# Moving 44 of 48 tile transposes from TensorE to the DMA engines, with a shorter layernorm, in a fused attention and MLP block

## The chip, the cores and the metric

One core of one Trainium2 chip runs the whole program. The metric is device microseconds from the first to the last instruction, as the runtime times an execution; the median of several executions is quoted. The profile's span is about 2 us shorter than that time (858.1 us beside 859.8 us).

## The reference, cut to what matters

```python
# x: 2048 x 1024, H = 32 heads of 32; bf16 everywhere
h  = x + linear_attention(layernorm(x), wqkv, wo)
#   q, k, v = layernorm(x) @ wqkv;  phi(t) = where(t > 0, t + 1, exp(t)) + 1e-6
#   kv = phi(k)^T v,  z = sum phi(k);  o = phi(q) kv / (phi(q) z + 1e-6);  o @ wo
h2 = h + (relu(n @ W_gate) * (n @ W_up)) @ W_down,   n = layernorm(h);   F = 3584
```

The matmuls of this kernel contract over partitions. The normalized `x`, the attention output and the normalized `h` come out with rows on partitions and must be turned, so that features lie on partitions, before the next matmul. That is 3 uses x 16 tiles of 128 x 1024 = 48 tile transposes.

## The kernel before

The kernel records its operations with the buffers that they read and write, and puts semaphore waits where they depend on another engine. A tile transpose is eight PE transposes of 128 x 128 into one PSUM bank and one copy out of it by ScalarE (ACT):

```python
def transpose8(src_ap, src_bufs, b, nblk, name):          # L461 in the profile of before
    tb = bank_bf(b)
    for i in range(nblk):
        PL.add("pe", lambda e, i=i: e.transpose(tb[:, i, :], src_ap[:, i*P:(i+1)*P], ident[:]), ...)
def evac_T(eng, b, nblk, dst_ap, dst_bufs, name):          # L469
    PL.add("act", lambda e: e.activation(out=dst_ap, in_=bank_bf(b)[:, 0:nblk, :], func=ACTF.Identity), ...)
```

`T1` turns the first layernorm's tiles (`xn` to `xnT`), `a3` the attention output (`osb` to `oT`), `a5` the second layernorm's tiles (`xn` to `hnT`). Between them, `a1` is a query projection, `a2` computes a tile's attention output, and `a4` its output projection, residual sum and second layernorm; `nop` is an empty place. Four stages follow one another:

```python
for st in range(WB): ...            # start: WB = 4 tiles, layernorm -> T1 -> first key projection
for st in range(WB, NST):           # projection: 12 steps
    T1(st + 1); ln1_norm(st + 2); ln1_stats(st + 3)
    trickle(2)                      # two of the later weight loads
    kvp(st); kvacc(st - 1)          # 32 matmuls of 512 columns, then 16 small ones
# first attention block: query projections a1 fill the gaps of this chain
chain = [("a2", 0), ("a2", 1), ("a2", 2), ("a3", 0), ("a2", 3), ("a3", 1), ("a4", 0), ("a3", 2),
         ("a4", 1), ("a3", 3), ("a5", 0), ("a4", 2), ("a5", 1), ("a4", 3), ("a5", 2), ("a5", 3)]
# MLP, 4 row blocks: gate/up units of 16 matmuls, with the next block's attention pieces between them,
# then two down-projection rounds
```

The layernorm takes mean and variance on VectorE (DVE), then three one-column operations on GpSimd (POOL), then normalizes on DVE. (In the cuts, SP is the engine that issues the DMA transfers.)

```python
pool: ve   = var + eps
pool: rstd = ve ** -0.5
pool: nmr  = mean * rstd * -1
dve:  xn   = x * rstd + nmr
```

## Time and profile before

| | before |
|---|---|
| median of 4 runs | 859.82 us (859.80 to 859.83) |
| profiled span | 858.1 us |
| TensorE busy / idle in the span | 845.4 us / 12.7 us |
| ACT, DVE busy | 174.2 us, 273.2 us |
| POOL busy, instructions | 35.6 us, 108 |
| DMA, mean | 128 GB/s |

A busy TensorE is not yet a bound, since matmuls overlap in the record (219 ns recorded for a transpose, 56 ns from one to the next).

### The profile page before, as it was taken

The page shows a single profiled execution, that of the slowest core. Times are in us where ns is not written, and L with a number is a line of the kernel's source. Part 1 is how long each engine was busy: PE and PEld are TensorE (multiplying, and loading weights), DVE is VectorE, ACT ScalarE, POOL GpSimd, SP SyncE. Part 2 cuts the span into 40 slices and gives each one's busy share as a digit, 9 for nine tenths or more (in the row PEclk, how much of TensorE's full clock was granted, in tenths as well). Part 3 has the DMA queues.
Part 4 walks back from the last instruction along what each step waited for, and adds up shares of the span by engine and source line. Part 5 has one row for each costly group of instructions (what it writes and reads, how often), then busy time and mean ns, then how long its engine had stood idle before and what let it go on. Part 6 is the DMA issues. An engine that isn't in the chain of part 4 may idle for free.

```text
span 858.1 us, 10919 instructions
## 1 busy us (share of the span) xinstructions
PE 845.4 (99%) x4538; PEld 407.1 (47%) x4627; DVE 273.2 (32%) x517; ACT 174.2 (20%) x262; POOL 35.6 (4%) x108
## 2 busy tenths in 40 slices
PE   7999999999999999999999999999999999999998
PEld 3555555544544444445444444544444444444443
DVE  6444524766433321124442101343411002112111
ACT  3344443324222210002222100022221001111100
POOL 3101100001000000000000000000000000000000
PEclk9999999999999999999999999999999999999999
DMA  9448100001233345553334465334344555363052
GB/s 295 135 147 272 61 2 1 1 13 38 89 121 123 111 160 183 177 166 99 123 123 148 147 196 173 122 112 151 97 157 154 189 173 163 107 197 98 29 170 95
DMA packets 105536, 109.75 MB, mean 128 GB/s; under 512 B 2960, under 2 KB 101520, under 8 KB 105488
## 3 DMA queue, kind: packets, MB, share of 16 engines
q1 hardware_dynamic: 105488, 109.06, 39.8%
q8 instruction: 36, 0.59, 0.3%
q14 instruction: 12, 0.10, 0.0%
HBM read 104.86 MB, written 4.19 MB: 127 GB/s over the span
## 4 chain that ended last, share of the span: by engine, by line
PE 96%; DVE 2%; issue 1%; POOL 1%; ACT 0%; DVEq 0%; ACTq 0%; POOLq 0%
PE ps L451 94%; PE ps L461 2%; DVE st L481 1%; POOL rstd L489 0%; DVE xn L504 0%; POOL nmr L492 0%; POOL ve L486 0%; DVE mv L484 0%; DVE RE L525 0%; DVE RF L693 0%; DVE RC L750 0%; ACT Et L520 0%; ACT RA L562 0%; POOL RF L344 0%; DVE RF L360 0%
## 5 line engine op out<-in xcount | busy, mean ns | idle before, releaser
L451 PE MATMUL ps<-RE,gring 128*128 128x512 bf16 x876 | 197.0, 379 | 1.2
L451 PE MATMUL ps<-RC,gring 128*128 128x512 bf16 x877 | 195.0, 379 | 1.0
L451 PE MATMUL ps<-wdring,RA 128*128 128x512 bf16 x877 | 193.0, 379 | 1.0
L723 ACT ACTIVATE RC<-ps 128x512 bf16<-128x512 f32 x112 | 66.9, 598 | 461.9 <-PE ps L451 461.9
L725 DVE TENSOR_TENSOR RA<-RC,ps 128x512 bf16<-128x512 bf16 x112 | 76.9, 687 | 262.1 <-PE ps L451 262.1
L451 PEld LDWEIGHTS ps<-wdring,RA 128*128 128x128 bf16 x896 | 87.7, 98 | 105.7
L451 PEld LDWEIGHTS ps<-RC,gring 128*128 128x128 bf16 x896 | 87.0, 98 | 102.9
L451 PEld LDWEIGHTS ps<-RE,gring 128*128 128x128 bf16 x896 | 86.4, 98 | 100.1
L451 PE MATMUL ps<-RB,RA 128*128 128x512 bf16 x496 | 111.3, 379 | 2.9 <-ACT RA L562 2.1
L451 PEld LDWEIGHTS ps<-RB,RA 128*128 128x128 bf16 x512 | 49.1, 98 | 58.8 <-ACT RA L562 2.6
L750 DVE TENSOR_TENSOR RC<-ps,RF 128x512 bf16<-128x512 f32 x32 | 20.1, 683 | 176.9 <-PE ps L451 176.9
L451 PE MATMUL ps<-wo,RE 128*128 128x512 bf16 x248 | 57.4, 379 | 0.4
L451 PE MATMUL ps<-RA,RC 128*128 128x512 bf16 x249 | 57.0, 379 | 0.4
L520 ACT ACTIVATE Et<-ps 128x512 bf16<-128x512 f32 x64 | 38.2, 597 | 84.7 <-PE ps L451 49.1
L522 DVE TENSOR_SCALAR E2t<-Et 128x512 bf16<-128x512 bf16 x64 | 18.5, 288 | 78.1 <-ACT Et L520 78.0
L451 PEld LDWEIGHTS ps<-wo,RE 128*128 128x128 bf16 x256 | 25.0, 98 | 30.2
L451 PEld LDWEIGHTS ps<-RA,RC 128*128 128x128 bf16 x256 | 24.3, 98 | 27.2
L693 DVE TENSOR_TENSOR RF<-ps,x 128x512 bf16<-128x512 f32 x32 | 22.1, 691 | 28.7 <-PE ps L451 28.5
L486 POOL TENSOR_SCALAR ve<-mv 128x1 f32<-128x1 f32 x32 | 7.1, 223 | 573.9 <-DVE mv L484 573.9
L469 ACT ACTIVATE RE<-ps 128x1024 bf16<-128x1024 bf16 x24 | 24.5, 1022 | 24.7 <-PE ps L461 24.7
L591 ACT ACTIVATE RE<-ps 128x512 bf16<-128x512 f32 x32 | 19.1, 597 | 36.3 <-PE ps L451 36.3
L525 DVE SCALAR_TENSOR_TENSOR RB<-ps,E2t 128x512 bf16<-128x512 f32 x32 | 22.1, 692 | 1.1
(50 smaller groups left out, 329.1 us busy)
## 6 DMA issues: line engine op xcount, KB each, us to landing
gring<-in_B_W_gate_dram SPq DMA_DIRECT2D x28, 1024.0 KB, 5.4
gring<-in_B_W_up_dram SPq DMA_DIRECT2D x28, 1024.0 KB, 7.5
wdring<-in_B_W_down_dram SPq DMA_DIRECT2D x56, 512.0 KB, 3.6
RB<-in_A_wqkv_dram SPq DMA_DIRECT2D x4, 1024.0 KB, 8.9
x<-in_A_x_dram SPq DMA_DIRECT2D x16, 256.0 KB, 2.6
out_dram<-RC SPq DMA_DIRECT2D x32, 128.0 KB, 3.6
RE<-in_A_x_dram SPq DMA_DIRECT2D x15, 256.0 KB, 2.8
RC<-in_A_wqkv_dram SPq DMA_DIRECT2D x2, 1024.0 KB, 6.8
```

The source lines that it names most:

```text
L451: lambda e: e.matmul(out_ap, lhsT, rhs, start=start, stop=stop, skip_group_check=skip),
L461: lambda e, i=i: e.transpose(tb[:, i, :], src_ap[:, i * P:(i + 1) * P], ident[:]),
L469: PL.add("act", lambda e: e.activation(out=dst_ap, in_=src, func=ACTF.Identity), reads=[B_bank[b]], writes=dst_bufs, name=name)
L481: PL.add("dve", lambda e, c=c: e.bn_stats(out=st6[:, k, c * 6:(c + 1) * 6], in_=src_full[:, c * BCH:(c + 1) * BCH]), reads=[src_chunk_bufs ...
L520: PL.add("act", lambda e: e.activation(out=Et[:, k, 0:w], in_=src, func=ACTF.Exp), reads=[B_bank[b]], writes=[B_E[k]], name=name + "_exp")
L522: PL.add("dve", lambda e: e.tensor_scalar(out=E2t[:, k, 0:w], in0=Et[:, k, 0:w], scalar1=1.0, scalar2=1e-6, op0=ALU.min, op1=ALU.add), rea ...
L525: PL.add("dve", lambda e: e.scalar_tensor_tensor(out=dst_ap, in0=src, scalar=C1, in1=E2t[:, k, 0:w], op0=ALU.add, op1=ALU.max), reads=[B_b ...
L591: PL.add("act", lambda e, b=b, j=j: e.activation(out=vv[:, slot, j * NW:(j + 1) * NW], in_=bank(b, NW), func=ACTF.Identity), reads=[B_bank ...
L693: PL.add("dve", lambda e, b=b, nt=nt: e.tensor_tensor(out=hsb[:, hs, j, nt * NW:(nt + 1) * NW], in0=bank(b, NW), in1=x2[:, xs, nt * NW:(nt ...
L723: PL.add("act", lambda e: e.activation(out=rg[:, k, :], in_=bank(ga, SBW), func=ACTF.Relu), reads=[B_bank[ga]], writes=[B_rg[k]], name="rg ...
L725: PL.add("dve", lambda e: e.tensor_tensor(out=hhT[:, ft, :], in0=rg[:, k, :], in1=bank(gb, SBW), op=ALU.mult), reads=[B_rg[k], B_bank[gb]] ...
L750: PL.add("dve", lambda e, j=j, k=k: e.tensor_tensor(out=outst[:, k, :], in0=bank(banks4[j], NW), in1=hsb[:, hs, j, dh * NW:(dh + 1) * NW], ...
```

## The change

The intent: take the transposes off the busiest engine, and give the layernorm a shorter path through POOL. Cut to its core:

```diff
-        NPK = 5
+        NPK = 4          # slots of phi(k) and v
+        NXN = 4          # slots of xn, 2 before
+        USE_DMA_T = True
...
-            PL.add("pool", ... ve = var + EPS)
+            PL.add("dve",  ... ve = var + EPS)
             PL.add("pool", ... rstd = ve ** -0.5)
-            PL.add("pool", ... nmr = mean * rstd * -1)
-            dve: xn = x * rstd + nmr
+            dve: xn = (x - mean) * rstd
...
+        def T1d(st):
+            PL.add("sp", lambda e: e.dma_start_transpose(xnT[:, :, st * P:(st + 1) * P], xn[:, k, :]), ...)
...     # a3, a5: the same with osb -> oT, xn -> hnT, issued right after a2 and a4
-        NDUM0, NDUM1 = 14, 5
+        NDUM0, NDUM1 = 12, 3      # warm-up matmuls
...     # projection, step st
-                T1(st + 1); ln1_norm(st + 2)
+                ln1_norm(st + 2); T1d(st + 2)
...     # first attention block
+            chain = [("a2", 0), ("a2", 1), ("a2", 2), ("a2", 3), ("nop", 0), ("nop", 0), ("nop", 0),
+                     ("a4", 0), ("a4", 1), ("a4", 2), ("a4", 3)]
+        tail_units = 8            # query projections kept for after the chain
...     # attention pieces between the MLP units
+                    order = [("a2", 0), ("a2", 1), ("a2", 2), ("a2", 3), ("nop", 0), ("nop", 0),
+                             ("a4", 0), ("a4", 1), ("a4", 2), ("a4", 3)]
```

The first four tiles (`st < WB`) keep their PE transposes. So 12 + 16 + 16 = 44 tile transposes move.

More of the change, by code (lines that the diff above doesn't have):

```diff
@@ L232, in bass_sequential_preLN__linear_attn_block__glu_gated_reglu__prompt_kernel @@
         jp_i = RF[:, 768:1024].bitcast(dt.int32)
-        xn = sb("xn", [P, 2, D], bf16)
+        xn = sb("xn", [P, NXN, D], bf16)
         Et = sb("Et", [P, 3, EW], bf16)
@@ L279, in bass_sequential_preLN__linear_attn_block__glu_gated_reglu__prompt_kernel @@
         sl_out = slots("dout_", NOS)
+        sl_tx = slots("dtx_", NXN)
+        sl_to = slots("dto_", NO)
         def bufs(name, n):
@@ L285, in bass_sequential_preLN__linear_attn_block__glu_gated_reglu__prompt_kernel @@
         B_x1 = [bufs("x1_%d_" % i, NBC) for i in range(NX1)]
-        B_xn = bufs("xn_", 2)
+        B_xn = bufs("xn_", NXN)
         B_xnT = [bufs("xnT%d_" % s_, 2) for s_ in range(NST)]
@@ L485, in layernorm @@
                    reads=B_st6[k], writes=[B_mv[k]], name=name + "_aggr")
-            PL.add("pool", lambda e: e.tensor_scalar(out=ve[:, k, :], in0=mv[:, k, 1:2], scalar1=EPS,
-                                                     scalar2=None, op0=ALU.add),
+            PL.add("dve", lambda e: e.tensor_scalar(out=ve[:, k, :], in0=mv[:, k, 1:2], scalar1=EPS,
+                                                    scalar2=None, op0=ALU.add),
                    reads=[B_mv[k]], writes=[B_ve[k]], name=name + "_ve")
@@ L491, in layernorm @@
                    reads=[B_ve[k], B_neghalf], writes=[B_rstd[k]], name=name + "_rstd")
-            PL.add("pool", lambda e: e.tensor_scalar(out=nmr[:, k, :], in0=mv[:, k, 0:1],
-                                                     scalar1=rstd[:, k, :], scalar2=-1.0,
-                                                     op0=ALU.mult, op1=ALU.mult),
-                   reads=[B_mv[k], B_rstd[k]], writes=[B_nmr[k]], name=name + "_nmr")
             def norm():
-                if norm_eng == "act":
-                    PL.add("act", lambda e: e.activation(out=dst_ap, in_=src_full, func=ACTF.Identity,
-                                                         scale=rstd[:, k, :], bias=nmr[:, k, :]),
-                           reads=list(src_chunk_bufs) + [B_rstd[k], B_nmr[k]], writes=[dst_buf],
-                           name=name + "_norm")
-                else:
-                    PL.add("dve", lambda e: e.tensor_scalar(out=dst_ap, in0=src_full, scalar1=rstd[:, k, :],
-                                                            scalar2=nmr[:, k, :], op0=ALU.mult, op1=ALU.add),
-                           reads=list(src_chunk_bufs) + [B_rstd[k], B_nmr[k]], writes=[dst_buf],
-                           name=name + "_norm")
+                PL.add("dve", lambda e: e.tensor_scalar(out=dst_ap, in0=src_full, scalar1=mv[:, k, 0:1],
+                                                        scalar2=rstd[:, k, :], op0=ALU.subtract, op1=ALU.mult),
+                       reads=list(src_chunk_bufs) + [B_mv[k], B_rstd[k]], writes=[dst_buf],
+                       name=name + "_norm")
             if defer:
@@ L542, in ln1_stats @@
             i = st % NX1
-            ln1_norms[st] = layernorm(x1[:, i, :], B_x1[i], xn[:, st % 2, :], B_xn[st % 2], "dve",
+            ln1_norms[st] = layernorm(x1[:, i, :], B_x1[i], xn[:, st % NXN, :], B_xn[st % NXN], "dve",
                                       "ln1_%d" % st, defer=True)
@@ L558, in T1 @@
             (b,) = alloc_banks(P1_POOL)
-            transpose8(xn[:, st % 2, :], [B_xn[st % 2]], b, NDC, "T1_%d" % st)
+            transpose8(xn[:, st % NXN, :], [B_xn[st % NXN]], b, NDC, "T1_%d" % st)
             if split and NDC >= 2:
@@ L569, in T1 @@
                 evac_T("act", b, NDC, xnT[:, :, st * P:(st + 1) * P], B_xnT[st], "evT1_%d" % st)
+        def T1d(st):
+            k = st % NXN
+            PL.add("sp", lambda e: e.dma_start_transpose(xnT[:, :, st * P:(st + 1) * P], xn[:, k, :]),
+                   reads=[B_xn[k]], writes=B_xnT[st], slot=sl_tx[k], name="T1d_%d" % st)
         def xnT_buf(st, dc):
@@ L679, in a3 @@
             k = o_slot_of[st]
+            if USE_DMA_T:
+                PL.add("sp", lambda e: e.dma_start_transpose(oT[:, :, j * P:(j + 1) * P], osb[:, k, :]),
+                       reads=B_o[k], writes=[B_oT[j]], slot=sl_to[k], name="T3d_%d" % st)
+                return
             (b,) = alloc_banks(pool)
@@ L699, in a4 @@
                 load_x2(st + 2)
-            layernorm(hsb[:, hs, j, :], B_h[hs][j], xn[:, st % 2, :], B_xn[st % 2], "dve", "ln2_%d" % st)
+            layernorm(hsb[:, hs, j, :], B_h[hs][j], xn[:, st % NXN, :], B_xn[st % NXN], "dve", "ln2_%d" % st)
         def a5(r, j, pool):
             st = r * STB + j
+            k = st % NXN
+            if USE_DMA_T:
+                PL.add("sp", lambda e: e.dma_start_transpose(hnT[r % 2][:, :, j * P:(j + 1) * P], xn[:, k, :]),
+                       reads=[B_xn[k]], writes=[B_hnT[r % 2][j]], slot=sl_tx[k], name="T5d_%d" % st)
+                return
             (b,) = alloc_banks(pool)
-            transpose8(xn[:, st % 2, :], [B_xn[st % 2]], b, NDC, "T5_%d" % st)
+            transpose8(xn[:, k, :], [B_xn[k]], b, NDC, "T5_%d" % st)
             evac_T("act", b, NDC, hnT[r % 2][:, :, j * P:(j + 1) * P], [B_hnT[r % 2][j]], "evT5_%d" % st)
@@ L804, in trickle, with T1any @@
                     bulk.pop(0)()
-        NDUM0, NDUM1 = 14, 5
+        NDUM0, NDUM1 = 12, 3
+        def T1any(st):
+            if USE_DMA_T and st >= WB:
+                T1d(st)
+            else:
+                T1(st)
         pe_dummies(NDUM0)
@@ L819, in bass_sequential_preLN__linear_attn_block__glu_gated_reglu__prompt_kernel @@
                 ln1_norm(st + 1)
+                if USE_DMA_T and st + 1 >= WB:
+                    T1d(st + 1)
             if st == 0:
@@ L833, in bass_sequential_preLN__linear_attn_block__glu_gated_reglu__prompt_kernel @@
             if nt == 1:
-                if WB < NST:
-                    T1(WB)
-                if WB + 1 < NST:
-                    ln1_norm(WB + 1)
-                if WB + 2 < NST:
-                    ln1_stats(WB + 2)
-        for st in range(WB, NST):
-            if st + 1 < NST:
-                T1(st + 1)
-            if st + 2 < NST:
-                ln1_norm(st + 2)
-            if st + 3 < NST:
-                ln1_stats(st + 3)
+                if USE_DMA_T:
+                    if WB + 1 < NST:
+                        ln1_norm(WB + 1)
+                        T1d(WB + 1)
+                    if WB + 2 < NST:
+                        ln1_stats(WB + 2)
+                else:
+                    if WB < NST:
+                        T1(WB)
+                    if WB + 1 < NST:
+                        ln1_norm(WB + 1)
+                    if WB + 2 < NST:
+                        ln1_stats(WB + 2)
+        for st in range(WB, NST):
+            if USE_DMA_T:
+                if st + 2 < NST:
+                    ln1_norm(st + 2)
+                    T1d(st + 2)
+                if st + 3 < NST:
+                    ln1_stats(st + 3)
+            else:
+                if st + 1 < NST:
+                    T1(st + 1)
+                if st + 2 < NST:
+                    ln1_norm(st + 2)
+                if st + 3 < NST:
+                    ln1_stats(st + 3)
             trickle(2)
@@ L861, in bass_sequential_preLN__linear_attn_block__glu_gated_reglu__prompt_kernel @@
                 a1(sb_, ct, ALL)
-        chain = [("a2", 0), ("a2", 1), ("a2", 2), ("a3", 0), ("a2", 3), ("a3", 1), ("a4", 0),
-                 ("a3", 2), ("a4", 1), ("a3", 3), ("a5", 0), ("a4", 2), ("a5", 1), ("a4", 3),
-                 ("a5", 2), ("a5", 3)]
+        if USE_DMA_T:
+            chain = [("a2", 0), ("a2", 1), ("a2", 2), ("a2", 3), ("nop", 0), ("nop", 0), ("nop", 0),
+                     ("a4", 0), ("a4", 1), ("a4", 2), ("a4", 3)]
+        else:
+            chain = [("a2", 0), ("a2", 1), ("a2", 2), ("a3", 0), ("a2", 3), ("a3", 1), ("a4", 0),
+                     ("a3", 2), ("a4", 1), ("a3", 3), ("a5", 0), ("a4", 2), ("a5", 1), ("a4", 3),
+                     ("a5", 2), ("a5", 3)]
         chain = [(k_, j) for (k_, j) in chain if j < STB]
+        tail_units = 8 if USE_DMA_T else 0
         nper = []
-        remaining = len(rest)
+        remaining = max(0, len(rest) - tail_units)
         for i in range(len(chain)):
@@ L876, in run_piece @@
                 a2(r, j, pool)
+                if USE_DMA_T:
+                    a3(r, j, pool)
             elif k_ == "a3":
@@ L880, in run_piece @@
                 a4(r, j, pool)
+                if USE_DMA_T:
+                    a5(r, j, pool)
             elif k_ == "a5":
@@ L899, in bass_sequential_preLN__linear_attn_block__glu_gated_reglu__prompt_kernel @@
             if r + 1 < NSB:
-                order = [("a2", 0), ("a2", 1), ("a2", 2), ("a3", 0), ("a2", 3), ("a3", 1), ("a4", 0),
-                         ("a3", 2), ("a4", 1), ("a3", 3), ("a5", 0), ("a4", 2), ("a5", 1), ("a4", 3),
-                         ("a5", 2), ("nop", 0), ("a5", 3)]
+                if USE_DMA_T:
+                    order = [("a2", 0), ("a2", 1), ("a2", 2), ("a2", 3), ("nop", 0), ("nop", 0),
+                             ("a4", 0), ("a4", 1), ("a4", 2), ("a4", 3)]
+                else:
+                    order = [("a2", 0), ("a2", 1), ("a2", 2), ("a3", 0), ("a2", 3), ("a3", 1), ("a4", 0),
+                             ("a3", 2), ("a4", 1), ("a3", 3), ("a5", 0), ("a4", 2), ("a5", 1), ("a4", 3),
+                             ("a5", 2), ("nop", 0), ("a5", 3)]
                 bgq = [(k_, r + 1, j) for (k_, j) in order if j < STB]
```

## The prediction

> **What bounds the kernel now.** I read the page's totals first, then the chain of waits, then the windows by stage, then the order of matmuls inside one stage.
>
> ```profile
> span 858.1 us, 10919 instructions
> PE 845.4 (99%) x4538; PEld 407.1 (47%) x4627; DVE 273.2 (32%) x517; ACT 174.2 (20%) x262; POOL 35.6 (4%) x108
> ...
> PE 96%; DVE 2%; issue 1%; POOL 1%; ACT 0%; DVEq 0%; ACTq 0%; POOLq 0%
> PE ps L451 94%; PE ps L461 2%; DVE st L481 1%; POOL rstd L489 0%; DVE xn L504 0%; POOL nmr L492 0%; POOL ve L486 0%; DVE mv L484 0%; DVE RE L525 0%; DVE RF L693 0%; DVE RC L750 0%; ACT Et L520 0%; ACT RA L562 0%; POOL RF L344 0%; DVE RF L360 0%
> ```
>
> L451 is the helper of all real matmuls, L461 that of the PE transposes. A busy share alone would not prove a bound, but the chain agrees: 96% of it lies on TensorE, and L461 is the only other TensorE line on it. The table by stage (start, steady projection, attention, MLP; columns: stretch, its length, busy time with counts of PE, PEld, DVE, ACT, POOL, then granted clock, DMA share, GB/s) shows where slack is:
>
> ```profile
> 8.30:18.10 9.80, 7.40 (x49) 3.48 (x49) 7.51 (x17) 4.76 (x10) 3.05 (x9) 1.00 1.09 355
> 18.10:131.50 113.40, 112.64 (x764) 59.30 (x780) 48.42 (x102) 46.61 (x70) 12.73 (x36) 1.00 0.38 124
> 131.50:215.00 83.50, 82.58 (x502) 41.61 (x510) 54.27 (x123) 28.33 (x43) 4.24 (x12) 1.00 0.04 14
> 215.00:852.00 637.00, 633.47 (x3187) 298.92 (x3250) 155.82 (x262) 92.12 (x137) 12.71 (x36) 1.00 0.44 139
> ```
>
> From 18 us to the end TensorE is idle under 1% of each stage while DMA has more than half its time free. Only in the first 18 us does PE wait. So a TensorE instruction taken away after 18 us shortens the program by what it occupies, not by its listed duration. What it occupies is read from the starts of the `ones`/kv group that recurs once per 128-row tile:
>
> ```profile
> 122.27 0.22 PE L451 MATMUL ps<-RE 128*128 128x128 bf16 x1
> ...
> 122.92 0.61 PE L461 MATMUL ps<-ident,xn 128*128 128x128 bf16 x8
> ...
> 130.27 0.22 PE L451 MATMUL ps<-RE 128*128 128x128 bf16 x1
> ...
> 137.82 0.22 PE L451 MATMUL ps<-RE 128*128 128x128 bf16 x1
> ```
>
> Tile to tile with a transpose group between is 130.27 - 122.27 = 8.00 us; the next step has none (the last tile was transposed already) and takes 137.82 - 130.27 = 7.55 us. One group of eight transposes costs 0.45 us of TensorE time, 56 ns each, not the 0.61 us of its record nor 8 x 219 ns. The chain of waits lists the same groups at 0.45 to 0.47 us.
>
> **What the Trainium skill says.** Four places bear on it.
> - "Trainium Kernel Development and Optimization", Performance Expectations: matmul busy time misleads because matmuls are pipelined. The trace agrees: 219 ns recorded per transpose, 56 ns occupied.
> - "VectorE: DVE Perf Modes", The three transpose paths: 390 ns for a 128x128 bf16 transpose on TensorE, 1309 ns through the DMA crossbar. The first figure does not hold in this pipelined stream (56 ns). The second has no counterpart in the trace before, which holds no DMA transpose.
> - "DMA: Bandwidth & Descriptors", Latency and other measured facts: 261 GB/s for a DMA transpose with a non-contiguous middle dimension.
> - "Advanced Engine Details and Errata", X-Bar Transpose (TRN2): transposes run about as fast as ordinary DMAs, 350 to 400 GB/s; no two streams of them may run at once. The change issues all from SP, so it keeps to that.
>
> These disagree on one 128x1024 tile (256 KB, eight blocks). At 261 GB/s it moves in 262144/261e3 = 1.0 us; in this trace a plain 256 KB load of x takes 2.6 us from issue to landing, so some 3 us. Eight blocks at 1309 ns one after another would be 10.5 us. I take 3 to 5 us as likely and 10 us as the bad case. All three are estimates.
>
> **The change part by part.**
> 1. *PE transposes removed.* 48 groups stand before: 16 tiles in each of three uses. After, the first four tiles of the first layernorm keep theirs; 12 + 16 + 16 = 44 groups go. All are later than 18 us, where PE is the bound: 44 x 0.45 = 19.8 us.
> 2. *ACT copies out of PSUM removed.* 44 of them at 1.02 us = 45 us. ACT is 20% busy and 0% of the chain, so 0 us directly.
> 3. *44 DMA transposes added on SP.* Off TensorE; they count only through arrival. Order and slack:
>    - Projection: tile st+2 is normalized and issued at the head of step st, so two steps of 7.55 us lie before its use, some 15 us. But 10.5 MB of weights trickle in over the first half of this stage, two loads of up to 1 MB per step; such loads land in 6.8 to 7.0 us here. A transpose of 3 to 5 us behind them still arrives.
>    - Attention of the first block, where nothing of the MLP can be put in between: the output tiles are transposed at once, and the first `a4` comes after the fourth `a2` and four query projections (4 x 1.73 = 6.9 us; eight matmuls of 0.216 us each). The tight spot is the last hidden tile: after its `a4` stand 1 + 8 projections, 9 x 1.73 = 15.5 us. Its layernorm takes (from the trace: 0.69 residual, 1.27 statistics, 0.21 aggregation, about 1 for the rest of the scalars, 0.55 normalize) about 4 us, which leaves 11 us for the DMA. DMA is 4% busy there. In the kernel before, TensorE lost 0.32 us at this place.
>    - MLP blocks: pieces follow one another by 3.45 us units; two empty places separate `a2` from `a4`, and the last hidden tile is done some 18 units (60 us) and two down-projection rounds before it is needed. 3, 5 or 10 us are hidden alike. It adds 2 MB beside 21 MB of weights per block.
> 4. *Layernorm scalars.* `ve` moves from POOL (223 ns) to DVE, `nmr` (268 ns plus a hand-over near 0.1 us) goes, and the normalize keeps its shape, so 546 ns. That shortens aggregate-to-normalize from about 1.4 to about 1.0 us. It can count only where PE waits for layernorm: the waits list 1.1 us of PE on `xn` in two waits and 2.1 us on the evacuation after it, all within the first 18 us. DVE is 7.51 of 9.80 us busy there and the first matmul waits for its weights at 8.14 us, so I allow 0.5 us, and 0.2 us at the 212 us place.
> 5. *Four dummy matmuls fewer.* They end at 6.04 us, before the first transpose at 6.79 us; 0 us.
> 6. *Buffers.* `xn` from 2 to 4, `pk`/`v` from 5 to 4. A `pk` slot is rewritten four tiles later, its reader is done after one. 0 us.
> 7. *New order of the chain*: `a2` pieces directly after one another. Each needs 1.8 us of DVE after it (0.19 + 0.35 + 2 x 0.69) plus two phi pairs of 0.98 us, in a step of 0.65 + 2 x 1.73 = 4.1 us: 3.8 us, just inside. An `a4` step is 5.2 us of PE against about 5.3 us of DVE, which eight banks absorb.
> 8. *New waits of TensorE on DMA semaphores*: hand-overs of about 0.05 us where the chain shows "issue", on a few tens of tiles: +0.3 us at most, plus a first wait here or there: I add 0.2 us for both.
>
> Sum: 859.8 - 19.8 - 0.5 - 0.2 + 0.2 = 839.5 us, that is 839.5/859.82 = 0.976, 2.4% faster.
>
> **The rivals.**
> - *Crossbar transposes are slow (10 us or more).* For it: 1309 ns times eight, and nothing in the trace measures one. Then projection needs about 12 x 10 us of DMA beside 0.38 x 113 = 43 us already used, 163 us in a 113 us stage if they take the engines alone: some 50 us lost, and the tail waits for four in a row. That makes 870 to 910 us. Against it: the two bandwidth figures, and the change keeps the PE path just for the first four tiles and adds eight projections as a cushion, as somebody who knows of a latency of several microseconds would.
> - *A wait takes the place of the work.* Latency of 6 to 9 us behind weight loads: PE starves in the first steps of projection and at the end of the first attention block, 1 to 3 us each, 842 to 848 us: "same". For it: 1.09 DMA share at 8 to 18 us, when the first transpose is issued. Against: it is not used until about 40 us.
> - *SP's queue stops behind a transpose that waits for the layernorm, and weights come late.* SP already sits waiting 470 us for PE and 222 us for the residual, and weights are fetched two blocks of 14 us ahead, so a few microseconds disappear. About 0 us.
> - *DVE becomes the bound in the first attention block* (54 of 83 us busy now, plus a small `ve`): under 1 us.
>
> **Range and chances.** The removed work is measured, so the lower end is close: 837.5. Above, the room is for stalls: 2% is reached at 842.6, so 3.1 us of unforeseen waiting turn "faster" into "same". I give 0.70 to faster, 0.18 to within 2%, 0.12 to slower (only the slow crossbar does that). The range 837.5 to 850 should hold it 8 times in 10.
>
> **What would show it.** Right: L461 has 32 matmuls left; the tile-to-tile step in projection is 7.55 us everywhere; TensorE's idle time after 18 us stays near 5 us; DMA transposes land in 3 to 5 us, their time on TensorE's list of waits near zero. Wrong: a step of 8 us or more that ends with a DMA into the transposed tiles; PE idle before the first gate matmul; transposes of 10 us or a DMA share near 1 in projection; fewer than 0.45 us gained per group.

## The result, and the profile after

The changed kernel takes 839.26 us (median of 8 runs, 838.92 to 840.97), the kernel before 859.81 us (13 runs). The ratio is 0.9762, with a 95% interval of 0.9752 to 0.9771. Such ratios divide the mean of one kernel's fast runs by the mean of the other's fast runs of the same rounds, so they are not quite the ratio of the medians. The output is correct.

The page of the changed kernel, with the helper of the real matmuls now at L455:

```profile
span 837.3 us, 10264 instructions
PE 825.1 (99%) x4187; PEld 387.3 (46%) x4271; DVE 278.5 (33%) x549; ACT 129.8 (16%) x218; POOL 19.3 (2%) x44
...
PE ps L455 95%; DVE RB L519 1%; ACT Et L514 1%; DVE E2t L516 0%; DVE kvm L621 0%; DVE zc L627 0%; DVE RE L519 0%; DVE RC L758 0%; ACTq L112 0%; DVE zsb L624 0%; DVEq L112 0%
```

TensorE is busy for 99% as before: the bound is the same engine with less to do, and no DMA stands on the chain. The table by stage (columns as in the prediction: stretch, length, busy time and counts of PE, PEld, DVE, ACT, POOL, granted clock, DMA share, GB/s):

```profile
18.10:126.00 107.90, 107.19 (x670) 53.83 (x682) 49.13 (x110) 34.04 (x57) 6.09 (x11) 1.00 0.59 159
126.00:205.00 79.00, 78.50 (x436) 37.90 (x444) 55.06 (x127) 20.91 (x35) 2.20 (x4) 1.00 0.19 41
205.00:831.00 626.00, 622.70 (x2997) 288.04 (x3057) 157.70 (x274) 67.57 (x113) 6.59 (x12) 1.00 0.51 152
```

TensorE idles 0.7, 0.5 and 3.3 us in the three by this table, no more than before, and part of that is matmul records that a trace lacks. DMA's share rose from 0.38 to 0.59 in projection. The group that recurs once per tile, in order of time:

```profile
124.30 0.22 PE L455 MATMUL ps<-RE 128*128 128x128 bf16 x1
...
131.85 0.22 PE L455 MATMUL ps<-RE 128*128 128x128 bf16 x1
```

The step is 7.55 us, which was the step without transposes in the kernel before. The issues of the DMA transposes, with count and median microseconds to landing:

```profile
RE<-RE SPq DMA_TRANSPOSE x16, 3.1
RA<-xn SPq DMA_TRANSPOSE x12, 3.5
RE<-xn SPq DMA_TRANSPOSE x8, 3.1
RC<-xn SPq DMA_TRANSPOSE x8, 3.1
```

Where the time came from, by the start of the same matmul in both timelines (fourth tile's first projection, next-to-last group of small matmuls, first gate matmul, end):

| point | before, us | after, us | gained | groups gone x 0.45 | rest |
|---|---|---|---|---|---|
| fourth tile starts | 18.06 | 17.45 | 0.6 | 0 | 0.6 |
| end of projection | 137.82 | 131.85 | 6.0 | 12: 5.4 | 0.6 |
| first gate matmul | 214.83 | 204.80 | 10.0 | 20: 9.0 | 1.0 |
| end of span | 858.1 | 837.3 | 20.8 | 44: 19.8 | 1.0 |

Every stage gains in proportion to the groups that left it. The rest of 1.0 us comes in the start and in the first attention block.

### The profile page after: what moved, and what is told of

It is laid out like the page before. It is cut to its first block, busy times and chain, and to the rows that moved or that the text cites.

```text
span 837.3 us, 10264 instructions
## 1 busy us (share of the span) xinstructions
PE 825.1 (99%) x4187; PEld 387.3 (46%) x4271; DVE 278.5 (33%) x549; ACT 129.8 (16%) x218; POOL 19.3 (2%) x44
## 2 busy tenths in 40 slices
DMA packets 151999, 121.27 MB, mean 145 GB/s; under 512 B 49424, under 2 KB 147984, under 8 KB 151952
## 4 chain that ended last, share of the span: by engine, by line
PE 95%; DVE 2%; ACT 1%; issue 1%; ACTq 0%; DVEq 0%
PE ps L455 95%; DVE RB L519 1%; ACT Et L514 1%; DVE E2t L516 0%; DVE kvm L621 0%; DVE zc L627 0%; DVE RE L519 0%; DVE RC L758 0%; ACTq L112 0%; DVE zsb L624 0%; DVEq L112 0%
## 5 line engine op out<-in xcount | busy, mean ns | idle before, releaser
L455 PE MATMUL ps<-RE,gring 128*128 128x512 bf16 x876 | 194.8, 379 | 1.1
L455 PE MATMUL ps<-RC,gring 128*128 128x512 bf16 x877 | 193.8, 379 | 1.0
L455 PE MATMUL ps<-wdring,RA 128*128 128x512 bf16 x877 | 193.0, 379 | 1.0
L455 PEld LDWEIGHTS ps<-wdring,RA 128*128 128x128 bf16 x896 | 87.7, 98 | 105.7
L455 PEld LDWEIGHTS ps<-RC,gring 128*128 128x128 bf16 x896 | 87.4, 98 | 104.8
L455 PEld LDWEIGHTS ps<-RE,gring 128*128 128x128 bf16 x896 | 87.0, 98 | 103.8
L455 PE MATMUL ps<-RB,RA 128*128 128x512 bf16 x497 | 112.3, 379 | 3.8 <-ACT RA L556 2.4
L455 PEld LDWEIGHTS ps<-RB,RA 128*128 128x128 bf16 x512 | 48.7, 98 | 60.0 <-ACT RA L556 2.7
L455 PE MATMUL ps<-wo,RE 128*128 128x512 bf16 x251 | 57.6, 379 | 0.3
L455 PE MATMUL ps<-RA,RC 128*128 128x512 bf16 x250 | 56.2, 379 | 0.3
L455 PEld LDWEIGHTS ps<-wo,RE 128*128 128x128 bf16 x256 | 25.0, 98 | 30.2
L455 PEld LDWEIGHTS ps<-RA,RC 128*128 128x128 bf16 x256 | 24.6, 98 | 29.0
L493 POOL TENSOR_TENSOR rstd<-ve,neghalf 128x1 f32<-128x1 f32 x32 | 17.7, 553 | 561.8 <-DVE ve L490 561.8
L519 DVE SCALAR_TENSOR_TENSOR RE<-ps,E2t 128x512 bf16<-128x512 f32 x32 | 22.1, 692 | 1.1
```

Source lines behind the costliest of these rows:

```text
L455: lambda e: e.matmul(out_ap, lhsT, rhs, start=start, stop=stop, skip_group_check=skip),
L493: PL.add("pool", lambda e: e.tensor_tensor(out=rstd[:, k, :], in0=ve[:, k, :], in1=neghalf[:], op=ALU.pow), reads=[B_ve[k], B_neghalf], wr ...
L519: PL.add("dve", lambda e: e.scalar_tensor_tensor(out=dst_ap, in0=src, scalar=C1, in1=E2t[:, k, 0:w], op0=ALU.add, op1=ALU.max), reads=[B_b ...
```

## The experiments

The theory: TensorE's own occupation by 44 groups is the gain, 0.45 us each; DMA time is hidden because every tile has some slack (by the prediction 6.9 us for the attention outputs, 11 us for the last hidden tile, 15 us in projection); the scalars are worth half a microsecond. The rivals: the gain comes from what went along with the transposes (evacuations, PSUM banks, waits, order, scalars); or it hangs on a latency that is only just short enough. Runs e1 to e4, e5 to e7 and e8 to e11 were taken on three different chips. All are compared with the changed kernel as e8 measured it, 839.25 us; its four runs there spread from 838.81 to 839.74 us, so a difference under some 0.5 us is not clear of noise.

### Transposes back on TensorE, all else changed (e1_pe_transposes)

```diff
-        USE_DMA_T = True
+        USE_DMA_T = False
```

> The changed kernel with all 48 transpose groups back on TensorE and the old order; the new layernorm scalars, the buffer counts and the fewer dummies stay. If the DMA transposes carry the gain (44 x 0.45 us), only the start gains and this takes 858.9 to 859.4 us. If scalars, buffers or order carried a good part of it, 850 us or less.

Measured: 859.15 us (12 runs; ratio to before 0.9993, interval 0.9984 to 1.0001). All but the DMA transposes and their order is worth 0.7 us by the medians, and the interval reaches 1. The DMA transposes are worth 859.15 - 839.25 = 19.9 us, where 839.25 us is the changed kernel measured again below.

### The old scalars with the DMA transposes (e2_old_scalars)

```diff
-            PL.add("dve",  ... ve = var + EPS);                        dve: xn = (x - mean) * rstd
+            PL.add("pool", ... ve = var + EPS); pool: nmr = -mean*rstd; dve: xn = x * rstd + nmr
```

> The changed kernel with the old layernorm scalars (sum with eps and the negated product on POOL, multiply-add normalize). If they matter only in the first 18 us, 839.9 us (0.6 us more than the changed kernel), up to 840.5 with the delay of the last transpose of the first attention block. If the shorter scalar path is what keeps the DMA transposes hidden, 843 us or more.

Measured: 839.66 us (839.65 to 839.67). That is 0.4 us more, which lies inside the spread of the changed kernel's own runs: what the scalars are worth is small, and not told from zero here. They do not keep the transposes hidden.

### Transposes that nobody reads, beside the DMA ones (e3_ghost)

```diff
+        def ghost(pool):
+            (b,) = alloc_banks(pool); tb = bank_bf(b)
+            for i in range(8):
+                PL.add("pe", lambda e, i=i: e.transpose(tb[:, i, :], ident[:], ident[:]), ...)
         def T1d(st):          # also at the head of a3 and a5
+            ghost(P1_POOL)
```

> The changed kernel, in which TensorE also runs eight transposes of the identity into a free PSUM bank at each of the 44 places, with nobody reading them. If what was saved is TensorE's occupation alone, this takes back 44 x 0.45 = 19.8 us: 859.1 us. If a good part of the gain came from the evacuations, the PSUM banks or the waits that went too, it stays at 850 us or less.

Measured: 858.60 us (20 runs, 857.96 to 858.98). With no evacuation, no reader and no wait on data, 44 groups cost 858.60 - 839.25 = 19.35 us, that is 0.44 us each. The ghosts still take a PSUM bank, but TensorE's list of waits holds none for a bank. The rival falls: the evacuations by ACT went (busy 174.2 to 129.8 us), and with the old order and the waits on data they are worth some 859.15 - 858.60 = 0.55 us. Half a microsecond of the 19.8 is not recovered; what it is made of was not looked for.

### The first layernorm's tiles on TensorE (e4_ln1_on_pe)

```diff
-                T1d(st + 2)        # projection, and the same at its start
+                T1(st + 1)         # before ln1_norm(st + 2), as in the kernel before
```

> The changed kernel with the first layernorm's 12 tiles transposed on TensorE again, the other 32 groups by DMA. If each group is worth 0.45 us, 839.3 + 12 x 0.45 = 844.7 us. If the gain is concentrated in the MLP part or in the first attention block, nearer 839.3; if the projection stage held most of it, above 848.

Measured: 844.40 us (844.33 to 844.60), 5.15 us more for 12 groups, 0.43 us each. The gain is spread evenly.

### Every DMA transpose twice, one after the other (e5_dma_twice)

The second has to wait for the first, as both write the same tile; so the time until a tile is there doubles, and SP's queue is held as long.

```diff
+            for _ in range(2):
                 PL.add("sp", lambda e: e.dma_start_transpose(...), slot=sl_tx[k], ...)   # all three places
```

> Every DMA transpose is issued twice, the second after the first has landed, so a tile takes about 6.2 us and SP is held that long. If the slack is as worked out (two steps in projection, 11 us at the last hidden tile), this is just hidden: 839.3 to 842 us; the tightest spots are projection, where 6.2 + 1.3 us of issuing meets a step of 7.55 us, and the last hidden tile, some 1 us before the first gate matmul. If latency is already close to the path, 845 us or more.

Measured: 844.21 us (844.08 to 844.68), 5.0 us more: outside what I expected. All of it is in projection; TensorE waits for no DMA in the attention and MLP parts. The matmuls of this kernel that waited for a DMA transpose:

```profile
98.21 7.08 PE L455 MATMUL ps<-RB,RA 128*128 128x512 bf16 x32 [3.29 <-DMA RA<-xn]
...
106.49 7.08 PE L455 MATMUL ps<-RB,RA 128*128 128x512 bf16 x32 [0.57 <-DMA RA<-xn]
...
114.87 5.35 PE L455 MATMUL ps<-RB,RA 128*128 128x512 bf16 x24 [0.67 <-DMA RA<-xn]
```

The chain of waits of the same run shows why:

```profile
56.39 7.96 DMA RA<-xn
64.36 1.23 SPq L568
65.60 0.04 issue
65.64 0.58 SPq L383
...
67.22 4.13 DMA RA<-xn
```

The first of a pair lands not in 3.1 but in 7.96 us, because two weight loads of up to 1 MB were issued just ahead of it on the same DMA engines. A pair and its loads then take 56.39 to 67.22, 10.8 us, against a step of 7.55 us, and the slack of two steps is used up after some tiles. My sum had put 3.1 us there twice. It is the doubling that brings the loads so close: they wait on SP for the second transpose and so stand right ahead of the next step's. In the changed kernel the loads go out at 49.39 us and the next transpose at 55.67 us; none took more than 5.1 us in projection, and the last tile, issued at 108.11 us, is used at 124.95 us.

### Every DMA transpose three times (e6_dma_three_times)

```diff
+            for _ in range(3):
```

> Every DMA transpose issued three times one after the other, about 9.3 us a tile: the slow crossbar of the prediction's first rival. If that rival's arithmetic is right, 870 to 910 us: about 20 us lost in projection (10.6 us per step against 7.55) and about 20 us before the first gate matmul. If the slack is larger than I think, below 850.

Measured: 954.80 us (2 runs), granted clock 0.957; neither 870 to 910 us nor below 850. TensorE's list of waits (waiter, what it waited for, microseconds, times, longest):

```profile
PE ps L455 <- DMA gring<-in_B_W_gate_dram: 27.7, 6, 9.6
PE ps L455 <- DMA RA<-xn: 25.6, 6, 7.8
PE ps L455 <- DVE RA L736: 19.7, 3, 6.6
PE ps L455 <- DMA RE<-xn: 15.0, 1, 15.0
```

The two waits that I had summed are there: 25.6 us on projection's tiles (20 expected) and 15.0 us before the first gate matmul (20 expected). Two things were missing. First, 27.7 us on gate weights: a queue that waits for one transpose before it issues the next issues the weights behind it late, as one of the prediction's rivals said, which it had put at 0 us. Secondly, the clock. The same 32 matmuls after a short and after a long gap:

```profile
88.85 7.08 PE L455 MATMUL ps<-RB,RA 128*128 128x512 bf16 x32 [2.06 <-DMA RA<-xn]
...
104.35 8.82 PE L455 MATMUL ps<-RB,RA 128*128 128x512 bf16 x32 [7.79 <-DMA RA<-xn]
```

After a gap of 7.79 us they take 8.82 instead of 7.08 us. In all TensorE is busy 854.5 us here and 829.9 us in the run with two transposes, with the same instructions, all 4271 of them recorded in both: 25 us are slower matmuls. The waits on DVE are the stopped queue once more. Before each of the three, DVE itself stood waiting for a residual tile of `x`, whose load SP had issued late, behind transposes:

```profile
318.41 1.29 DVE L698 TENSOR_TENSOR RF<-ps,x 128x512 bf16<-128x512 f32 x2 [11.31 <-DMA x<-in_A_x_dram]
...
323.32 13.74 PE L455 MATMUL ps<-RE,gring 128*128 128x512 bf16 x56 [6.59 <-DVE RA L736]
```

So loads that came late cost TensorE 27.7 + 19.7 = 47.4 us of waiting, more than the 25.6 + 15.0 = 40.6 us for the transposes themselves.

### The cushion taken away (e7_no_cushion)

```diff
-        tail_units = 8 if USE_DMA_T else 0
+        tail_units = 0
```

> The eight query projections kept for the end of the first attention block are spread over the chain instead, so two (3.45 us) stand after the last a4. The last transpose lands 7.2 us after that a4, so TensorE should idle 3.8 us there: 843.1 us, with a wait on the transposed hidden tile in the list. If the cushion is not needed, 839.3 us.

Measured: 844.69 us (843.90 to 845.58), 5.4 us more. The last transpose's issue on SP, and TensorE's first gate matmuls:

```profile
205.46 1.23 SPq L709 DMA_TRANSPOSE RE<-xn  x1
```

```profile
201.57 3.62 PE L455 MATMUL ps<-RA,RC 128*128 128x512 bf16 x16
208.63 5.14 PE L455 MATMUL ps<-RE,gring 128*128 128x512 bf16 x16 [3.44 <-DMA RE<-xn]
```

and the windows around it:

```profile
204.00:208.00 4.00, 1.19 (x6) 0.34 (x4) 2.42 (x6) 0.74 (x2) 0.55 (x1) 1.00 0.47 112
208.00:212.00 4.00, 3.37 (x9) 1.26 (x10) 0.00 (x0) 0.00 (x0) 0.00 (x0) 0.57 0.02 4
```

The transpose lands 208.63 - 205.46 = 3.2 us after its issue; the wait is 3.44 us where 3.8 was expected. The other part is again the clock: it falls to 0.57 in the next 4 us, and 16 matmuls that take 3.62 us at full clock take 5.14 us. So the cushion of eight query projections is worth 5.4 us: 3.4 of waiting, 1.5 of clock, and 0.4 to 0.5 that was not traced. With it, the changed kernel's last tile is normalized at 192.58 and issued at 193.16 us, for a first gate matmul at 204.80:

```profile
192.58 0.55 DVE L498 TENSOR_SCALAR xn<-RF,mv,rstd 128x1024 bf16<-128x1024 bf16 x1 [0.80 <-POOL rstd L493]
...
193.16 1.23 SPq L709 DMA_TRANSPOSE RE<-xn  x1
...
204.80 3.62 PE L455 MATMUL ps<-RE,gring 128*128 128x512 bf16 x16
```

That is 11.6 us for a transfer of 3.1 us.

### Fewer tiles through TensorE at the start (e8 to e11)

If a group is worth 0.45 us and the start also waits for evacuations, fewer than four first tiles should do better. One number is changed, and the changed kernel is run once more beside it.

```diff
-        WB = min(4, NST)
+        WB = min(3, NST)        # e9;  2 in e10, 1 in e11
```

> The changed kernel once more, to stand beside the next three on the same chip: 839.3 us.

> Only three tiles of the first layernorm go through TensorE before the others start. One start-up step has 1.73 us of matmuls, 0.45 us of transposes and about 0.9 us in which TensorE waits for the evacuation; with the DMA the last two go: 1.3 us less, 838.0 us, if the fourth tile arrives before its first matmul, 10 us later. If it does not, or the weights come later than needed, 839.3 or more.

> The same with two tiles: 2.6 us less, 836.7 us, if the third tile and the last weight chunk (landing near 20 us) are in time; the last chunk is needed near 21 us. If the weights become the bound of the start, 838 to 841 us.

> The same with one tile. The four weight chunks are then needed at 8.3, 10, 11.7 and 13.5 us but land up to 20 us: I expect the start to wait for weights and lose what it gained, 840 to 845 us. If weights are not the limit, 835.4 us.

| run | median, us | range, us | ratio to before (95%) |
|---|---|---|---|
| e8, four tiles (the changed kernel) | 839.25 | 838.81 to 839.74 | 0.9761 (0.9747 to 0.9774) |
| e9, three | 838.02 | 837.46 to 838.21 | 0.9745 (0.9732 to 0.9759) |
| e10, two | 836.47 | 836.34 to 836.87 | 0.9728 (0.9715 to 0.9741) |
| e11, one | 844.41 | 842.69 to 844.72 | 0.9816 (0.9803 to 0.9830) |

The ranges of four and three tiles do not overlap, nor those of three and two, though the intervals of the ratios do. The start of the kernel with two tiles:

```profile
8.75 1.90 PE L455 MATMUL ps<-RB,RA 128*128 128x512 bf16 x8 [0.81 <-DMA RB<-in_A_wqkv_dram]
10.49 0.61 PE L465 MATMUL ps<-ident,xn 128*128 128x128 bf16 x8
11.83 12.26 PE L455 MATMUL ps<-RB,RA 128*128 128x512 bf16 x56 [0.73 <-ACT RA L556]
```

After the second tile nothing waits any more: the third comes by DMA and is in time. In the changed kernel two further starts of that kind follow, at 13.03 and 16.11 us, each with a wait of 0.7 to 1.0 us. With one tile TensorE's waits hold what was feared:

```profile
PE ps L455 <- DMA RB<-in_A_wqkv_dram: 5.1, 4, 2.5
```

Weights bound the start then, and the clock fell with the waits:

```profile
12.70 2.54 PE L455 MATMUL ps<-RB,RA 128*128 128x512 bf16 x8 [2.46 <-DMA RB<-in_A_wqkv_dram]
16.34 3.60 PE L455 MATMUL ps<-RB,RA 128*128 128x512 bf16 x8 [1.10 <-DMA RB<-in_A_wqkv_dram]
```

Eight such matmuls take 1.90 us at full clock; here the granted clock was 0.73 from 12 to 16 us and 0.50 from 16 to 20 us, which makes 2.3 us more in these two groups. The kernel with two first tiles is the best, at 836.47 us: 2.7% faster than before, 0.3% faster than the change.

## Why the prediction was right

It said 839.5 us; 839.26 us was measured. The mechanism held, and so did the signs that it named: 7.55 us from tile to tile, 32 transposes left on TensorE, TensorE idle for 4.5 us after 18 us. That the sum is only 0.24 us off is partly luck, since its small terms are not known that well. By its own steps:

1. *PE transposes removed, 19.8 us*: right, and the step that carries the sum. Taking them back cost 19.9 us with evacuations (e1) and 19.35 us without (e3); 12 of them cost 5.15 us, 5.4 by the rule (e4); the MLP part shrank by 10.8 us for 24 groups. Reading the difference of two recurring steps gave the right size; the recorded durations would have given 44 x 0.61 = 27 us, or 44 x 8 x 0.219 = 77 us.
2. *ACT copies, 0 us*: right; 44.4 us of ACT went, e3 shows that they are worth nothing.
3. *Latency 3 to 5 us, hidden*: right for the kernel as it is; medians 3.1 and 3.5 us. The first layernorm's ranged from 3.0 to 5.1 us, the attention outputs' up to 7.9 us, none on TensorE's list of waits. The slack in projection was put at some 15 us and was 16.8 us for the last tile; the slack for the last hidden tile was put at 11 us and was 11.6 us. One allowance was too small: the step gave a transpose behind weight loads 3 to 5 us, and in e5 one right behind two of them landed after 8 us.
4. *Scalars, 0.7 us in two places*: 0.4 us by e2, not clear of noise; the timelines show 1.0 us in those places, and e1, which has the fewer dummies and the other buffers too, 0.7 us. Small, and right within that. One reading behind it was wrong: of TensorE's two waits on `xn`, together 1.1 us, only the one of 0.75 us lies in the first 18 us; the other is the 0.32 us at 212 us, which the step counts again as its second place.
5. *Dummies and buffers, 0 us*: not separated from the scalars; together 0.7 us by e1. The reason given holds for the first 14 dummies alone. The five of the second group run from 7.23 to 8.47 us in the kernel before, after the first transpose. With three of them the first real matmul starts at 8.22 instead of 8.31 us, as it then waits 0.62 us for its weights.
6. *New order, within DVE's reach*: right; TensorE idles 0.5 us in the first attention block. (By the prediction's table it was 0.92 of 83.5 us there before, 1.1%, not under 1% as it says of each stage.)
7. *New waits, +0.2 us*: no wait on a transpose is listed at all.

The rivals: the slow crossbar did not come; what it would cost was mis-sized. 9.3 us a tile made 955 us, not 870 to 910, since late loads (47.4 us of waiting for weights and, through DVE, for `x`) and the lowered clock (25 us) were left out. The stopped queue, put at about 0 us, is 0 at 3.1 us a tile and a main loss at 9.3. The middle rival, 6 to 9 us at 842 to 848 us, was tried as 6 us and gave 844.2.

The clock is stated in the Trainium skill, "TensorE: Matmul & The Clock Gate", Why this matters for your kernels, which asks for no TensorE gaps above about 3 us. The runs agree that gaps of this order can cost the clock, and show no fixed limit. After a gap of 3.29 us (e5) 32 matmuls took 7.08 us, as after 2.06 us (e6); after 3.44 us (e7) 16 of them took 5.14 instead of 3.62 us; but in e11 a gap of 2.46 us was enough. Of the four runs of e5 two had a mean clock of 1.0 and two of 0.998, so one program does not always lose it. The rivals should have been priced with it.

## What to carry to other kernels

Where one engine bounds the program, price an instruction by the difference between two otherwise equal steps with and without it, not by its record. Work moved to DMA was free here as long as each transfer had more slack than its latency *behind the loads in front of it*, and the order of the program, here two empty places and eight projections kept back, is what bought that slack. A queue that waits for one transfer also holds back the loads behind it, which in e6 cost more than the transposes did. Where slack runs out on TensorE, add to the wait itself some 1.5 to 2.3 us for the clock: the gap of 3.44 us in e7 and those of 2.46 and 1.10 us in e11 cost that much, though one of 3.29 us in e5 cost nothing in the profiled run.

## What the Trainium skill lacked or had wrong

- "VectorE: DVE Perf Modes", The three transpose paths: 390 ns for a 128 x 128 transpose on TensorE and 1309 ns by DMA are no measure of what either costs in a stream. Back to back on TensorE one occupied 55 to 56 ns (19.35 us for 352 in e3); eight blocks in one DMA landed in 3.0 us at the least and 3.1 to 3.5 us in the median, not in eight times 1309 ns, as the prediction's bad case had it.
- "DMA: Bandwidth & Descriptors", Latency and other measured facts: 261 GB/s for a DMA transpose. Here the DMA share rose in projection from 0.38 of 113.4 us to 0.59 of 107.9 us, 20.6 us for 12 transposes, so about 1.7 us of all 16 engines each; 262 KB in that time is some 150 GB/s. This is an estimate from those two rows and rather a floor: the share reaches 1.09 elsewhere in the same tables, so it counts packets that overlap. No run measured the bandwidth of a transpose by itself.
- "Advanced Engine Details and Errata", X-Bar Transpose (TRN2): "as fast as regular DMAs" holds for the latency (3.1 us beside 2.8 us for a plain 256 KB load of x) and not for the rest: SP took 1.23 us (median) to issue one, 0.34 us for a plain load of x, and each added (151999 - 105536)/44 = 1056 packets. No page gives the issue time of such a transpose, 128 x 1024 from SBUF to SBUF, on this chip.
- "TensorE: Matmul & The Clock Gate", Why this matters for your kernels: a limit of about 3 us on the gap is too simple. A gap of 2.46 us lowered the clock in e11, and one of 3.29 us left it at 1.0 in the profiled run of e5. The price was 1.5 us after a gap of 3.44 us and 1.7 us after one of 7.79 us.
